# Loading x earlier, narrower first V products, matmuls on zeros and an earlier memory update in an attention and gMLP block on one core

## The chip, the cores and the metric

The kernel runs on one core of a Trainium2 chip. The metric is the device time of one execution in microseconds (us). Ratios are computed as the mean time of one kernel's runs over the mean of the other kernel's runs of the same rounds, so a ratio is not quite the ratio of the medians that are quoted beside it.

## The reference

The block has two halves. The first is attention with a compressive memory (32 heads of 32, four segments of 512 tokens); the second is a gMLP. The change touches the first half only.

```python
x = A_x                                   # 1 x 2048 x 1024, bfloat16
h  = x + attn(layernorm(x))               # below
h2 = h + gmlp(layernorm(h))               # gelu, layernorm, 2048x2048 spatial mix, w_out

# attn, per head; q, k, v = x @ wq, x @ wk, x @ wv, cut into 4 segments of 512
M, z = 0, 0
for s in range(4):
    logits = qs @ ks.T * scale + mask     # local, causal
    a_dot  = softmax(logits) @ vs
    a_mem  = phi(qs) @ M / (phi(qs) @ z + 1e-6)
    outs.append(g * a_mem + (1 - g) * a_dot)
    M = M + phi(ks).T @ vs                # the memory update
    z = z + phi(ks).sum(0)
return concat(outs) @ wo
```

## The kernel before

The kernel is written for five instruction streams (TensorE `pe`, ScalarE `act`, VectorE `dve`, GpSimd `pool`, SyncE `sp`, which issues all DMAs). A recorder derives every semaphore wait from the bytes and PSUM banks that an instruction touches. Each stream runs in program order, so the order in which the Python code calls things is the order in which each engine meets them. Each segment is worked off in eight iterations `c` of four heads; `n = 8 s + c`.

The prologue loads x and weights and prepares segment 0:

```python
x_load(0)
x_load(1)
sp.dma_start(WV[:, :, 0:512], wcols(A_wv, 0, 512))
x_load(2)
x_load(3)
sp.dma_start(WK[:, :, 0:256], ...)
sp.dma_start(WQ[:, :, 0:256], ...)
sp.dma_start(BETAB[:], ...)
sp.dma_start(WV[:, :, 512:1024], ...)
sp.dma_start(WK[:, :, 256:D], ...)
sp.dma_start(WQ[:, :, 256:D], ...)
sp.dma_start(WO[:], wcols(A_wo, 0, D))          # 2 MB, needed in segment 1
# ... cut ...
stats_of(0)                                     # bn_stats on DVE, rsqrt on POOL
stats_of(1)
for tc in range(4):
    o = ln_apply(XCH[tc], ks[tc])               # DVE
    if tc < 2:
        stats_of(tc + 2)
    pe_T(XNT[0], tc, o)                         # 8 transposes on PE, copy on ACT
    proj_v(0, tc, 0)                            # 8 matmuls 128x512, copy on ACT
gates()                                         # gate and MASKG, on DVE
proj_qk(0, 1); proj_qk(0, 0); phi(0)            # phi(n): DVE, then a DMA transpose into PK
rot["banks"] = [6, 7]                           # all fills below share two PSUM banks
```

The loop. `logits(n, r)` is four to eight small matmuls into banks 0 to 3 and an exp on ScalarE (`e_106`, `e_107`, `e_108` for r = 0, 1, 2). `fill` does whole projections of 8 matmuls (K and Q of the next iteration, V, or the output projection `wo` of the segment before); each takes the next bank of the two. `mem(n)` and `mem_norm(n)` (`rdm`, `tm`) read the memory inside the third logits. `state(n)` is the memory update:

```python
if s < NSEG - 1 and c < 4:
    x_load(4 * (s + 1) + c)                     # x of the next segment, used in this iteration
    ln_tasks(XCH[c], XNT[(s + 1) % 2], c)
logits(n, 0); fill(f1)                          # f1: K of n + 1
if n > 0: pv(n - 1, 2)                          # ends with norm(n - 1) on DVE
bg_pop()                                        # one step of up to three layer norms, on DVE
logits(n, 1); fill(f2)                          # f2: Q of n + 1
pv(n, 0)
logits(n, 2)                                    # with mem(n), mem_norm(n) from segment 1 on
fill(f3)
if n < LAST: phi(n + 1)
pv(n, 1)
bg_pop()
state(n)
fill(f4)                                        # empty in segment 0
bg_pop()

def state(n):                                   # not in the last segment
    b = next_bank()
    for tcl in range(4):
        pe.matmul(PS[:, b, 0:132], PK[n % 3][:, tcl, :], V[...], ...)
    dve ... MSUM[:, c, :] (+)= PS[:, b, 0:132]  # frees the bank
    dve ... MZB[:, c] = MSUM[:, c] * MASKG[:, c]
```

The softmax here doesn't subtract the row's maximum and nothing guards it: scores larger than these inputs give would overflow.

## Time and profile before

The median is 827.59 us (827.46 to 829.17). This is how the span of 825.4 us in its profiled execution divides, by the start of the first logits of an iteration in the timeline:

| stretch | from, us | length, us |
|---|---|---|
| prologue | 0 | 28.79 |
| iteration 0 | 28.79 | 7.62 |
| rest of segment 0 (n = 1 to 7) | 36.41 | 54.61 |
| segments 1 and 2 (n = 8 to 23) | 91.02 | 167.83 |
| segment 3 and the gMLP | 258.85 | 566.55 |

From the page of the kernel before, the span and the engines' busy time:

```profile
span 825.4 us, 12334 instructions
PE 787.2 (95%) x5258; PEld 384.3 (47%) x5344; DVE 368.6 (45%) x753; ACT 301.8 (37%) x351; POOL 120.8 (15%) x234
```

TensorE bounds the kernel as a whole; 38 us are left in which it is idle. What it waited for between 25 and 262 us, from the waits of PE (total us, times, longest; a line of 2.5 us called "issue" and lines of 0.7 us and less are left out):

```profile
PE ps L209 <- DVE hch_86 L209: 3.0, 3, 1.3
PE ps L209 <- DVE msum L209: 2.9, 5, 0.8
PE ps L209 <- DVE hch_87 L209: 2.7, 2, 1.9
PE ps L209 <- DVE hch_85 L209: 2.5, 3, 1.1
PE ps L209 <- ACT v L209: 1.1, 4, 0.3
```

All of the lines shown are waits for a PSUM bank that another engine has not emptied yet: `hch` is the residual add of the output projection, `msum` the update, `v` the copy of V. How such a wait comes about is seen in iteration 10. First TensorE, then VectorE, from the timeline (start, duration, what, and the idle time before it with its cause):

```profile
119.75 0.40 PE L209 MATMUL ps<-v,pk_104 128*128 128x132 bf16 x4
121.30 0.38 PE L209 MATMUL ps<-wo,oT 128*128 128x512 bf16 x1 [1.15 <-DVE hch_85 L209]
```

```profile
117.71 1.42 DVE L209 BATCH_NORM_STATS2 stats_61<-xch_94 128x6 f32<-128x512 bf16 x2 [1.08 <-DMA xch_94<-in_A_x_dram]
119.29 0.12 DVE L209 TENSOR_SCALAR rdm<-ps 128x16 f32<-128x16 f32 x1
119.73 0.69 DVE L209 TENSOR_TENSOR tm<-ps,rdm 128x512 f32<-128x512 f32 x1
120.34 0.68 DVE L209 TENSOR_TENSOR hch_85<-xr_83,ps 128x512 bf16<-128x512 bf16 x1
```

The second `wo` fill (121.30) has the bank of the first, because the update took the other one. The waits of DVE between 30 and 262 us:

```profile
DVE stats_60 L209 <- DMA xch_93<-in_A_x_dram: 7.7, 3, 3.6
DVE stats_59 L209 <- DMA xch_92<-in_A_x_dram: 7.6, 2, 5.0
DVE stats_61 L209 <- DMA xch_94<-in_A_x_dram: 5.5, 3, 3.2
DVE stats_62 L209 <- DMA xch_95<-in_A_x_dram: 3.1, 1, 3.1
```

### The profile page before, as it was taken

Reading aid. Unit: us, or ns where it says so; the run is one execution under the profiler, and the core shown is the slowest. Engines: PE = TensorE matmul, PEld = TensorE weight load, DVE = VectorE, ACT = ScalarE, POOL = GpSimd, SP = SyncE. Lnnn points to the kernel's source line nnn. Section 1 sums busy time; section 2 is a strip of 40 time slices with the busy share of each in tenths; the row PEclk is TensorE's granted clock in tenths of the full one; section 3 lists DMA queues with packets and bytes.
Section 4 is the critical chain, followed back from the end, with each engine's and each line's share of the span. In section 5 each row is a group of like instructions: output and inputs, shape, how many; then the busy total and the mean of one; then the engine's idle time right before and its main releaser. Section 6 shows DMA issues by size and latency. Waiting matters only on the chain.

```text
span 825.4 us, 12334 instructions
## 1 busy us (share of the span) xinstructions
PE 787.2 (95%) x5258; PEld 384.3 (47%) x5344; DVE 368.6 (45%) x753; ACT 301.8 (37%) x351; POOL 120.8 (15%) x234
## 2 busy tenths in 40 slices
PE   4899998998899999999999999999999999999998
PEld 2445444444444555455554444444444444444443
DVE  4454568756775568564456000043233314323432
ACT  2788866776667876133333333200000000000000
POOL 2143233323332233000033000000000000000000
PEclk9999999999999999999999999999999999999999
DMA  8631344344422224841013400190170035012002
GB/s 276 218 81 34 78 91 114 65 87 93 116 65 53 45 84 123 200 106 52 3 50 96 83 1 1 57 243 1 56 155 0 7 91 114 0 52 58 0 8 84
DMA packets 124808, 64.79 MB, mean 78 GB/s; under 512 B 94800, under 2 KB 113744, under 8 KB 124752
## 3 DMA queue, kind: packets, MB, share of 16 engines
q1 hardware_dynamic: 124752, 63.99, 31.2%
q8 instruction: 42, 0.69, 0.3%
q14 instruction: 14, 0.11, 0.1%
HBM read 32.51 MB, written 8.39 MB: 50 GB/s over the span
## 4 chain that ended last, share of the span: by engine, by line
PE 80%; DVE 9%; DMA 5%; ACT 3%; issue 2%; SPq 1%; POOL 0%
PE ps L209 80%; DMA xch_93<-in_A_x_dram 1%; DMA xch_95<-in_A_x_dram 1%; DMA xch_94<-in_A_x_dram 1%; DMA wv<-in_A_wv_dram 1%; ACT e_108 L209 1%; DVE stats_60 L209 1%; DVE stats_62 L209 1%; DVE rdm L209 1%; SPq L209 1%; ACT v L209 1%; DVE tm L209 1%; ACT etmp L209 1%; DVE etmp L209 1%; DVE stats_59 L209 1%
## 5 line engine op out<-in xcount | busy, mean ns | idle before, releaser
L209 PE MATMUL ps<-w_out,yT 128*128 128x512 bf16 x439 | 96.9, 379 | 0.5
L209 PE MATMUL ps<-wspT_119,z_117 128*128 128x512 bf16 x439 | 96.5, 379 | 0.5
L209 PE MATMUL ps<-wspT_120,z_117 128*128 128x512 bf16 x439 | 96.5, 379 | 0.5
L209 ACT ACTIVATE e_106<-ps 128x2048 bf16<-128x2048 f32 x32 | 60.0, 1874 | 36.2 <-PE ps L209 36.2
L209 PEld LDWEIGHTS ps<-wspT_119,z_117 128*128 128x128 bf16 x448 | 43.8, 98 | 52.8
L209 PEld LDWEIGHTS ps<-wspT_120,z_117 128*128 128x128 bf16 x448 | 43.8, 98 | 52.9
L209 PEld LDWEIGHTS ps<-w_out,yT 128*128 128x128 bf16 x448 | 43.8, 98 | 52.9
L209 PE MATMUL ps<-wo,oT 128*128 128x512 bf16 x243 | 57.2, 379 | 8.7 <-DVE hch_86 L209 3.0
L209 DVE TENSOR_TENSOR tmpg_126<-ps,brow_124 128x512 f32<-128x512 f32 x14 | 9.7, 690 | 117.6 <-DMA brow_124<-in_B_b_sp_dram 97.3
L209 ACT ACTIVATE z_117<-ps 128x448 bf16<-128x448 f32 x64 | 34.8, 544 | 74.7 <-PE ps L209 74.7
L209 ACT ACTIVATE e_107<-ps 128x2048 bf16<-128x2048 f32 x32 | 60.1, 1877 | 0.5 <-PE ps L209 0.5
L209 ACT ACTIVATE z1T<-ps 128x512 bf16<-128x512 f32 x56 | 33.4, 597 | 63.3 <-PE ps L209 63.3
L209 DVE BATCH_NORM_STATS2 zst<-z_117 128x6 f32<-128x448 bf16 x64 | 39.1, 620 | 32.6 <-ACT z_117 L209 32.6
L209 POOL TENSOR_SCALAR_AFFINE_SELECT e_107<-e_107 128x512 bf16<-128x512 bf16 x64 | 39.6, 643 | 46.9 <-ACT e_107 L209 46.9
L209 PEld LDWEIGHTS ps<-wo,oT 128*128 128x128 bf16 x256 | 23.6, 98 | 33.5 <-DVE hch_86 L209 3.3
L209 POOL TENSOR_SCALAR_AFFINE_SELECT e_106<-e_106 128x512 bf16<-128x512 bf16 x32 | 20.3, 634 | 126.9 <-ACT e_106 L209 126.9
L209 PE MATMUL ps<-wv,xnT_77 128*128 128x512 bf16 x121 | 30.5, 396 | 7.0 <-ACT xnT_77 L209 3.7
L209 ACT ACTIVATE e_108<-ps 128x1024 bf16<-128x1024 f32 x32 | 32.7, 1023 | 10.5 <-PE ps L209 10.3
L209 PE MATMUL ps<-xnT_78,wk 128*128 128x512 bf16 x125 | 29.7, 380 | 2.1 <-DVE msum L209 1.6
L209 ACT ACTIVATE v<-ps 128x512 bf16<-128x512 f32 x32 | 19.1, 597 | 34.4 <-PE ps L209 34.4
L209 PE MATMUL ps<-xnT_77,wk 128*128 128x512 bf16 x125 | 29.7, 380 | 2.0 <-DVE msum L209 1.3
L209 PE MATMUL ps<-xnT_77,wq 128*128 128x512 bf16 x120 | 28.8, 380 | 1.2 <-issue 0.8
(206 smaller groups left out, 1068.0 us busy)
## 6 DMA issues: line engine op xcount, KB each, us to landing
w_out<-in_B_w_out_dram SPq DMA_DIRECT2D x1, 3584.0 KB, 13.4
wv<-in_A_wv_dram SPq DMA_DIRECT2D x2, 1024.0 KB, 7.4
wo<-in_A_wo_dram SPq DMA_DIRECT2D x1, 2048.0 KB, 16.6
xr_83<-in_A_x_dram SPq DMA_DIRECT2D x8, 256.0 KB, 3.0
xr_84<-in_A_x_dram SPq DMA_DIRECT2D x8, 256.0 KB, 3.1
win_114<-in_B_w_in_dram SPq DMA_DIRECT2D x2, 896.0 KB, 5.5
wk<-in_A_wk_dram SPq DMA_DIRECT2D x1, 1536.0 KB, 10.0
wq<-in_A_wq_dram SPq DMA_DIRECT2D x1, 1536.0 KB, 12.8
```

The source lines that it names most:

```text
L209: ins = getattr(e, op.name)(*op.args, **op.kw)
```

## The change

It has four parts. The first V products are made in quarter widths and loaded so, with layer norms of chunks 0 and 1 ahead of later statistics, to start the first logits sooner; twelve matmuls on zeros run before any data is there, to raise TensorE's clock. (One early exp on ScalarE stands in the diff too; ScalarE's table load is at 0.79 us in both profiles.) x is loaded a segment ahead. The mask of the gates moves into iteration 0. And the update moves up, to right after the third logits, which also gives the two fills of an iteration different banks.

```diff
-    x_load(0)
-    x_load(1)
-    sp.dma_start(WV[:, :, 0:512], wcols(A_wv, 0, 512))
-    x_load(2)
-    x_load(3)
+    for tc in range(4):
+        x_load(tc)
+    sp.dma_start(WV[:, :, 0:256], wcols(A_wv, 0, 256))
+    sp.dma_start(WV[:, :, 256:512], wcols(A_wv, 256, 512))
 ...                                         (WK, WQ first 256 columns, BETAB, second half of WV)
-    sp.dma_start(WK[:, :, 256:D], ...)
-    sp.dma_start(WQ[:, :, 256:D], ...)
-    sp.dma_start(WO[:], ...)
 ...
+    dve.memset(ETMP[:], 0.0)
+    act.activation(RDM[:, 0, 0:1], MHALF[:], ACTF.Exp)
 ...
+    for i in range(12):
+        pe.matmul(bank(7), IDENT[:], ETMP[:, 0, :], start=True, stop=True)
     stats_of(0)
     stats_of(1)
+    late = {1: [(0, 0)], 2: [(1, 0)], 3: [(2, 0), (0, 1), (1, 1), (3, 0), (2, 1), (3, 1)]}
+    lns = [ln_apply(XCH[0], ks[0]), ln_apply(XCH[1], ks[1])]
     for tc in range(4):
-        o = ln_apply(XCH[tc], ks[tc])
         if tc < 2:
             stats_of(tc + 2)
-        pe_T(XNT[0], tc, o)
-        proj_v(0, tc, 0)
+        pe_T(XNT[0], tc, lns[tc])
+        if tc in (1, 2):
+            lns.append(ln_apply(XCH[tc + 1], ks[tc + 1]))
+        for t_, q in late.get(tc, []):
+            proj_v_cols(0, t_, 256 * q, 256)
+    for tc in range(4, 8):
+        x_load(tc)
+    sp.dma_start(WK[:, :, 256:D], wcols(A_wk, 256, D))
+    sp.dma_start(WQ[:, :, 256:D], wcols(A_wq, 256, D))
+    sp.dma_start(WO[:], wcols(A_wo, 0, D))
 ...
         if s < NSEG - 1 and c < 4:
-            x_load(4 * (s + 1) + c)
             ln_tasks(XCH[c], XNT[(s + 1) % 2], c)
+        if s < NSEG - 2 and c >= 4:
+            x_load(4 * (s + 2) + c - 4)
 ...
         logits(n, 2)
+        if n == 0:
+            mask_g()
+        else:
+            state(n)
         fill(f3)
 ...
         bg_pop()
-        state(n)
+        if n == 0:
+            state(n)
         fill(f4)
```

## The prediction

> **What bounds the kernel.** TensorE is busy 95% of 825.4 us (page, part 1). After 345 us no TensorE gap over 0.1 us is left and the change touches nothing there, so only the first 260 us count. Timeline and waits, by stage:
> - Prologue: first logits at 28.79 us. LN of chunk 1 waits in VectorE's order behind the statistics of chunk 2 (x chunk landing at 10.8), and first V waits 2.3 us for its 1 MB weight load. Matmuls at 10.27-13.2 are spaced 427 ns, from 15.7 on 216 ns[...].
> - Segment 0: 7.65 us an iteration, TensorE and ScalarE nearly tied (ScalarE idles 0.8 us, before the V copy). Iterations 2-4 take 7.9-8.1: VectorE waits for x chunks (2-5 us each), frees the PV banks late.
> - Segments 1 and 2: 83.7 and 84.1 us. TensorE waits for hch evacuation 8.2 us in 8 places (second output-projection half takes the bank of the first), for msum about 3 us, for v about 1 us.

> **What changes.**
> 1. Prologue compute. Quarter V, LN of chunks 0 and 1 before later statistics and warm-up matmuls: adding up the trace's durations (statistics 1.6, LN 0.5, transposed copy 1.0, warm quarter V 0.9) gives first logits near 23.4, 5.4 us earlier.
> 2. But the queue. Four x chunks (1 MB) now precede the rest of WK, WQ and WO, all before the transpose that the first memory update needs. Packets after 14 us move at about 380 GB/s; WO's last moved at 30.5. An extra 1.05 MB puts it at about 33.4, and the transpose, issued near 24.5, stands behind it. ([...]here a transpose issued at 338.1 shows no packets until the weight load ahead of it ended near 342.) It lands near 35, against 33.3 before, when the update ran at 36.1 without waiting. So TensorE stalls 4-5 us at the first update; iteration 1 starts near 35.6 against 36.41. Kept: 0.8 us[...].
> 3. x a segment ahead takes VectorE's x waits (27 us in all) away; TensorE gets about 1 us in segment 0, and part of item 4.
> 4. Update at the third logits. In segments 1-2 the two fills of an iteration get different banks, and the second waits for msum, whose chain (e_108 exp, rdm, tm, msum) ends 2.7 us after mem, 0.3 after TensorE is ready. Output-projection iterations 10.3-11.7 -> 9.9-10.4; V iterations unchanged to -0.35. Both segments together -6 us. In segment 0 ScalarE's V copy now comes 0.27 us later in a ScalarE-tied loop: 7.65 -> 7.9 in most iterations, +2 us.

> **Sum.** -0.8 + 0.6 - 1 - 6 + 2, about -5.5: predicted 822 us, 80% range 815.5 to 826.5. Chances: faster by over 2% 0.06, within 2% 0.93, slower 0.01.

> **Signs.** Right: logits near 23-24 us; a TensorE wait of 3-6 us on the pk transpose before iteration 1; iterations of segment 0 near 7.9; no hch waits of a microsecond in segments 1-2 but waits on msum of 0.2-0.4; segments near 81; no x wait on VectorE after 30 us. After 345 us everything shifted only.

> **What would make it wrong.** If the transpose overtakes WO, 5 us more are kept (about 817). If VectorE, with 10.0-10.5 us of work in iterations with two layer norms, falls behind, msum comes late and the segments gain only 2-3 us. If ScalarE's slack hides the moved update, 2 us more.

The allowance for TensorE's clock in the stall was not worked out from any trace. The sum keeps that allowance as its term +0.6: all five terms come to -5.2, and without it they come to -5.8. The predicted 822 us was made with it.

## The result, and the profile after

The changed kernel takes 822.00 us (820.99 to 823.47) against 827.53 in the same rounds; the ratio is 0.9931 (95% interval 0.9908 to 0.9955), within 2%. From its page:

```profile
span 819.4 us, 12417 instructions
PE 792.0 (97%) x5302; PEld 390.7 (48%) x5388; DVE 373.9 (46%) x754; ACT 302.6 (37%) x356; POOL 120.8 (15%) x234
```

| stretch | before, us | after, us | difference |
|---|---|---|---|
| prologue | 28.79 | 23.31 | -5.48 |
| iteration 0 | 7.62 | 12.00 | +4.38 |
| rest of segment 0 | 54.61 | 56.49 | +1.88 |
| segments 1 and 2 | 167.83 | 161.08 | -6.75 |
| segment 3 and the gMLP | 566.55 | 566.52 | -0.03 |

**The prologue's 5.5 us come back as a stall.** The waits of PE, 25 to 262 us, changed kernel:

```profile
PE ps L209 <- DVE msum L209: 4.7, 16, 0.4
PE ps L209 <- DMA pk_103<-pqk_99: 4.2, 1, 4.2
PE ps L209 <- ACT e_106 L209: 2.2, 8, 0.7
```

The second line is one wait, in TensorE's timeline at the end of iteration 0:

```profile
30.20 0.56 PE L209 MATMUL ps<-v,e_107 128*128 128x33 bf16 x16
34.98 0.40 PE L209 MATMUL ps<-v,pk_103 128*128 128x132 bf16 x4 [4.23 <-DMA pk_103<-pqk_99]
35.31 0.39 PE L209 MATMUL ps<-qk_97 32*128 32x512 bf16 x4
35.64 3.44 PE L209 MATMUL ps<-xnT_77,wk 128*128 128x512 bf16 x8
```

Iteration 1 starts at 35.31 us against 36.41 before: only 1.1 us are left. The DMA view of 14 to 36 us gives the time from issue to landing, first of the kernel before, then of the changed one:

```profile
wo<-in_A_wo_dram SPq DMA_DIRECT2D x1, 2048.0 KB, 16.6
pk_103<-pqk_99 SPq DMA_TRANSPOSE x1, 3.2
```

```profile
wo<-in_A_wo_dram SPq DMA_DIRECT2D x1, 2048.0 KB, 18.6
pk_103<-pqk_99 SPq DMA_TRANSPOSE x1, 10.3
```

The transpose was issued at 30.07 before and at 24.58 after. It landed at 33.3 and 34.9: issued 5.5 us sooner, it arrived 1.6 us later. WO, issued at 15.61, landed at 34.2 (15.61 + 18.6); before, at 31.5 (14.89 + 16.6), 1.4 us after the transpose was issued.

**After the stall the clock was at one half.** The last timeline line shows eight matmuls of 128x512 in 3.44 us, where the same group took 1.90 in other iterations. TensorE in stretches of 3.41 us, changed kernel (us, PE busy and instructions, granted clock, DMA share, GB/s):

```profile
5.11:8.52 3.41, 1.65 (x14) 1.00 1.04 309
8.52:11.94 3.42, 2.67 (x16) 0.50 1.20 291
32.41:35.83 3.42, 0.85 (x9) 1.00 0.54 74
35.83:39.24 3.41, 3.41 (x17) 0.50 0.43 84
```

**Segments 1 and 2.** No `hch` or `v` wait is left in the list; instead there are 16 short ones for `msum` (the first line of the waits above). The place shown before, iteration 10, on VectorE and then TensorE:

```profile
117.09 1.41 DVE L209 BATCH_NORM_STATS2 stats_61<-xch_94 128x6 f32<-128x512 bf16 x2
119.32 0.17 DVE L209 TENSOR_SCALAR rdm<-ps 128x16 f32<-128x16 f32 x1 [0.57 <-ACT e_108 L209]
120.42 0.28 DVE L209 TENSOR_TENSOR msum<-msum,ps 128x132 f32<-128x132 f32 x1
```

```profile
120.76 1.04 PE L209 MATMUL ps<-wo,oT 128*128 128x512 bf16 x4 [0.18 <-DVE msum L209]
```

The statistics no longer wait for x; VectorE now waits for `e_108`, which it needs for the memory read.

### The profile page after: what moved, and what is told of

Read it like the earlier page. It is cut to its first block, busy times and chain, and to the rows that moved or that the text cites. A ratio compares the mean times of both kernels' runs of the same rounds, so it can differ in the third digit from the quotient of the medians.

```text
span 819.4 us, 12417 instructions
## 1 busy us (share of the span) xinstructions
PE 792.0 (97%) x5302; PEld 390.7 (48%) x5388; DVE 373.9 (46%) x754; ACT 302.6 (37%) x356; POOL 120.8 (15%) x234
## 4 chain that ended last, share of the span: by engine, by line
PE 83%; ACT 8%; DVE 6%; issue 2%; DMA 2%; POOL 0%
PE ps L209 83%; ACT e_106 L209 3%; ACT e_108 L209 3%; DVE tm L209 2%; DMA pk_103<-pqk_99 1%; DVE rdm L209 1%; ACT v L209 1%; ACT etmp L209 1%; DVE stats_61 L209 0%; DVE stats_62 L209 0%; DVE msum L209 0%; DMA xch_92<-in_A_x_dram 0%; DVE hch_85 L209 0%; DVE etmp L209 0%; DVE lno_89 L209 0%
## 5 line engine op out<-in xcount | busy, mean ns | idle before, releaser
L209 ACT ACTIVATE z1T<-ps 128x512 bf16<-128x512 f32 x56 | 33.4, 597 | 63.3 <-PE ps L209 63.3
L209 PE MATMUL ps<-wv,xnT_77 128*128 128x512 bf16 (+1 forms) x154 | 29.8, 343 | 1.5 <-DVE msum L209 1.2
L209 ACT ACTIVATE v<-ps 128x512 bf16<-128x512 f32 (+1 forms) x36 | 19.8, 550 | 29.3 <-PE ps L209 29.3
L209 PE MATMUL ps<-wv,xnT_78 128*128 128x512 bf16 x120 | 28.5, 379 | 1.5 <-DVE msum L209 1.2
## 6 DMA issues: line engine op xcount, KB each, us to landing
wo<-in_A_wo_dram SPq DMA_DIRECT2D x1, 2048.0 KB, 18.6
```

The lines of the kernel that those rows point to most:

```text
L209: ins = getattr(e, op.name)(*op.args, **op.kw)
```

## The experiments

In the lines below from experiments the buffer numbers are missing from the tile names; `pk` is `pk_103` to `pk_105`, and so on. Stage lengths and start times are from one profiled execution of each kernel. The start of the first logits goes with the clock of that execution. In the four profiles with the old prologue (e3, before, e4, e10) it lies at 28.09, 28.79, 29.55 and 31.03 us, where the record of full clock begins at 13.85, 14.41, 18.49 and 19.93. In the six with the twelve zeros it lies between 23.31 and 25.04. e1, e2, e5 and e7 ran on one chip, e3, e4, e6 and e8 on another, e7_again, e9 and e10 together. Every kernel gave correct output.

The theories at the start: (Q) the prologue's gain is eaten by the order of the DMA queue; (S) in segment 0 the earlier update costs time, because ScalarE and TensorE are tied there; (B) the banks are what shortens segments 1 and 2. The rivals: the transpose is late for reasons of its own; 7.89 us has other causes; and the waits for x, not the banks, were the cost in segments 1 and 2.

### e1_wo_late: the changed kernel with WO behind the first transpose

```diff
-    sp.dma_start(WO[:], wcols(A_wo, 0, D))      # before gates()
 ...
     phi(0)
+    sp.dma_start(WO[:], wcols(A_wo, 0, D))
```

> The changed kernel, with the load of WO issued after the transpose that the first memory update waits for, instead of ahead of it. Theory (the queue keeps the order of issue, so the transpose stands behind 2 MB of WO): the transpose lands near 29 to 31 us instead of 35, the 4.23 us TensorE wait before the first update is gone or under 1 us, iteration 1 starts near 31 instead of 35.31 and stays at the full clock; time near 816.5, 5 to 6 us below the changed kernel. Rival (the transpose is late for its own reasons, such as the gates' mask work on VectorE or sharing of the DMA engines): the wait stays over 3 us and the time near 822.

Measured: 817.32 us (817.07 to 818.01) against 828.11, ratio 0.9874. From its DMA view of 14 to 36 us:

```profile
wo<-in_A_wo_dram SPq DMA_DIRECT2D x1, 2048.0 KB, 9.8
pk<-pqk SPq DMA_TRANSPOSE x2, 3.6
```

The wait before the first update is gone (iteration 0 takes 7.62 us). Iteration 1 starts at 32.62 us, not near 31, because in this profile the first logits came at 25.00 instead of 23.31; in it the granted clock is 0.50 from 12.31 to 15.72 us, see e9. Theory Q holds, its rival falls. The gain, about 4.7 us between the medians of the changed kernel and of e1 (817.32 and 822.00, different rounds), is a little under the 5 to 6 expected. All four executions of e1 have a mean granted clock of 0.998, so probably all of them had one such stretch (half of 3.41 us is 0.002 of the span of 815.8); that would explain the missing part. Of the two transposes in the view, the first took 3.3 us from issue to landing. The second, issued at 34.02, now stands behind WO, which landed at 37.4 (27.62 + 9.8); it landed at 38.0, and TensorE waits 0.21 us for it in iteration 1. A later transpose costs 0.36 us in iteration 7.

### e2_seg0_late: the update of segment 0 back at the end

```diff
         if n == 0:
             mask_g()
-        else:
+        elif s > 0:
             state(n)
 ...
-        if n == 0:
+        if s == 0:
             state(n)
```

> The changed kernel with the memory update of segment 0 back at the end of the iteration; segments 1 and 2 keep it at the third logits. Theory (ScalarE and TensorE are tied in segment 0, and the moved update delays the V copy by 0.27 us): iterations 2 to 7 return from 7.89 to 7.65 us, the time falls 1.5 to 2 us, to about 820.3. Rival (7.89 comes from other work, such as layer norms now running at other times): iterations stay near 7.9 and the time near 822.

Measured: 820.28 us (817.84 to 820.97), ratio 0.9904. Iterations 2 to 7 take 7.65 us each (42.87, 50.52, 58.17, ... us), as expected, against 7.89. The reason is visible in ScalarE's timeline. First the kernel before, iteration 5, then the changed kernel, iteration 5, then e2, iteration 5:

```profile
75.18 0.60 ACT L209 ACTIVATE v<-ps 128x512 bf16<-128x512 f32 x1 [0.80 <-PE ps L209]
```

```profile
75.74 0.60 ACT L209 ACTIVATE v<-ps 128x512 bf16<-128x512 f32 x1 [1.03 <-PE ps L209]
```

```profile
72.94 0.60 ACT L209 ACTIVATE v<-ps 128x512 bf16<-128x512 f32 x1 [0.79 <-PE ps L209]
```

This is the only larger idle time of ScalarE in such an iteration. In the changed kernel the update runs on TensorE before V, so V, its copy and everything after it on ScalarE come later, and TensorE then waits 0.23 us for `e_106` at the second logits. Theory S holds: the stages show it. (The profile is the fastest of four executions whose other three lie at 820.15 and above; its clock stayed up after the stall. Its transpose, issued at 26.32 us behind WO, took 8.5 us to land.)

### e5_old_start: the changed kernel with the old compute of the prologue

```diff
-    (12 matmuls on zeros, quarter-width V, lns ahead)
+    for tc in range(4):
+        o = ln_apply(XCH[tc], ks[tc])
+        if tc < 2:
+            stats_of(tc + 2)
+        pe_T(XNT[0], tc, o)
+        proj_v(0, tc, 0)
```

> The changed kernel with the compute of its prologue as in the kernel before (no matmuls on zeros, V of the first half at once, layer norms in the old order); the loads keep their new order. Theory (the queue sets the end of iteration 0): first logits 2 to 4 us later than 23.31, the wait for the transpose shrinks by as much, iteration 1 starts within 0.5 us of 35.31, and the time is 820.5 to 822.5, perhaps 1 us under the changed kernel, as a shorter wait leaves the clock up. Rival (the earlier start is kept in the end): 2 to 4 us slower than the changed kernel, 824 to 826.

Measured: 821.29 us (820.55 to 821.82), ratio 0.9921. The first logits come at 28.37 us, 5.1 us later than in the changed kernel (more than the 2 to 4 expected), the wait for the transpose vanishes, iteration 1 starts at 36.00 (0.7 us later than in the changed kernel; I had expected at most 0.5), and its clock stays up: from there to segment 1 it takes 54.97 us instead of 56.49.

```profile
35.67 0.40 PE L209 MATMUL ps<-v,pk 128*128 128x132 bf16 x4
```

Taking out the whole compute part of the new prologue does not make the kernel slower. The rival falls; together with e1 this shows that in the changed kernel the queue, and not the compute before it, decided when iteration 0 could end.

### e3_update_only and e4_x_only: one part each, on the kernel before

e3 is the kernel before with the placement of the update alone. e4 is the kernel before with x a segment ahead alone:

```diff
 e3:     logits(n, 2)
+        if n > 0:
+            state(n)
         fill(f3)
 ...
-        state(n)
+        if n == 0:
+            state(n)

 e4:     phi(0)
+        for tc in range(4, 8):
+            x_load(tc)
 ...
-            x_load(4 * (s + 1) + c)
             ln_tasks(XCH[c], XNT[(s + 1) % 2], c)
+        if s < NSEG - 2 and c >= 4:
+            x_load(4 * (s + 2) + c - 4)
```

> The kernel before with the placement of the memory update alone (third logits, except in iteration 0); x chunks still load in the iteration that uses them. Theory (the exchange of banks is what shortens segments 1 and 2, but msum is then behind the VectorE wait for x in the first four iterations of each): segments 1 and 2 take 81 to 82.5 us instead of 83.7 and 84.1, segment 0 grows by 1 to 2 us, time 824 to 826. Rival (the x waits were what cost the time, and the placement only helps with them gone): segments 1 and 2 stay within 1 us, time 828 to 830.

> The kernel before with x a segment ahead alone: chunks 4 to 7 are loaded after the first transpose and later ones in the second half of a segment; the update stays last and the prologue's loads and compute are as before. Theory: segment 0's iterations 2 to 4 return to 7.65 us (1 us gained); in segments 1 and 2 the hch waits stay, shortened from 1.2-1.9 to 0.6-0.8 us in the first two output-projection iterations, and msum waits stay in part; each segment gains 1 to 2 us; time 823.5 to 825.5. Rival (the bank exchange is all): segments 1 and 2 unchanged, time 826.5 to 827.

Measured: e3 830.81 us (829.31 to 834.89), ratio 1.0050 (1.0022 to 1.0078): slower than the kernel before. e4 821.41 us (821.12 to 822.55), ratio 0.9931 (0.9916 to 0.9946): the same ratio as the whole change. Both of my expectations missed, e3 by 5 us and e4 by 2, in opposite directions.

| | rest of segment 0, us | segments 1 and 2, us |
|---|---|---|
| before | 54.61 | 167.83 |
| e3, update alone | 57.80 | 167.40 |
| e4, x alone | 53.55 | 163.57 |
| after, both (with the new prologue) | 56.49 | 161.08 |

The update alone saves 0.4 us in segments 1 and 2. The waits of PE, 25 to 262 us, in e3, then in e4:

```profile
PE ps L209 <- DVE msum L209: 14.4, 19, 2.0
```

```profile
PE ps L209 <- DVE hch L209: 5.4, 8, 0.8
PE ps L209 <- DVE msum L209: 1.1, 2, 0.6
```

In e3 the `hch` waits are gone, as the exchange of banks intends, but longer waits for `msum` stand in their place. An example from iteration 11 of e3, VectorE, then TensorE:

```profile
132.43 1.42 DVE L209 BATCH_NORM_STATS2 stats<-xch 128x6 f32<-128x512 bf16 x2 [1.85 <-DMA xch<-in_A_x_dram]
135.06 0.28 DVE L209 TENSOR_TENSOR msum<-msum,ps 128x132 f32<-128x132 f32 x1
```

```profile
135.40 1.90 PE L209 MATMUL ps<-wo,oT 128*128 128x512 bf16 x8 [1.75 <-DVE msum L209]
```

With x late, VectorE is late for whatever bank it has to empty next, and moving the update only changes which bank that is. In segment 0 it even adds a wait: the K fill of iterations 2 to 4 waits 1.0 to 1.2 us for `msum`, which the old order did not put in front of it. With x early (e4) VectorE's own waits for x after 30 us fall to one of 4.2 us (26.5 us in e3), and both kinds of TensorE's wait shrink: `hch` from 8.2 us to 5.4, `msum` from 2.9 to 1.1. So theory B in its strong form falls, and so does its strong rival. The early x is the main part, and the placement of the update is worth something in segments 1 and 2 only on top of it: 163.57 to 161.08, 2.5 us.

### e6_both, e7_update_before_third and e8_no_zeros

e6 is e1 and e2 together. e7 is e6 with the update of segments 1 and 2 one place further up; the product with the mask has to stay behind the memory read, since it overwrites what that reads:

```diff
         pv(n, 0)
+        if s > 0:
+            state(n)                       # matmuls, and MSUM += on VectorE
         logits(n, 2)
         if n == 0:
             mask_g()
         elif s > 0:
-            state(n)
+            mzb(n)                         # MZB = MSUM * MASKG
```

e8 is e7 without the twelve matmuls on zeros.

> e1 and e2 together: WO behind the first transpose and the update of segment 0 at the end of the iteration. Theory (two separate causes that add up): 5 us from the queue and 1.7 from segment 0, time 815 to 816; against it e7 has the earlier update of segments 1 and 2 alone, so e7 should be 5 to 6 us below. Rival (with the stall gone the later start of segment 0 gives the rest back, and e7's gain is mostly elsewhere): 817 or more.

> e1 and e2 together, and in segments 1 and 2 the update's matmuls one place earlier, ahead of the third logits (the product with the mask stays behind them). Theory (each second fill there waits 0.3 us for msum behind the normalisation of the memory read): those 16 waits go, iterations of segments 1 and 2 fall from 9.93-10.08 to 9.65-9.8, and the time is about 810.5: 5.5 from the queue, 1.7 from segment 0, 4.5 from here. Rival (ScalarE or VectorE bounds those iterations as well): near 815, as the first two parts alone.

> e7 without the twelve matmuls on zeros. There is no stall in e7 that could hide the prologue, so what they are worth must show. Theory (they raise the clock before V's first products, though a cold stretch can come back in the gaps): first logits 1 to 2.5 us later than 23.34, time 810.5 to 812. Rival (the gaps of the prologue lower the clock again whatever came first, so they are worth nothing on average): within 0.5 us of e7's 809.5.

| kernel | median, us | lowest to highest | ratio to before (95%) | segments 1 and 2, us |
|---|---|---|---|---|
| e6 | 814.47 | 813.63 to 815.22 | 0.9848 (0.9831 to 0.9864) | 160.83 |
| e7 | 809.53 | 808.69 to 810.36 | 0.9779 (0.9764 to 0.9795) | 155.92 |
| e8 | 809.81 | 808.69 to 811.02 | 0.9789 (0.9774 to 0.9803) | 155.94 |

e6: the queue and segment 0 add up; it lies a little under the 815 to 816 expected. e7: iterations of segments 1 and 2 fall from between 9.93 and 10.08 us to between 9.59 and 9.74 (iterations 8, 12 and 20, where ScalarE or VectorE is late for another reason, from 10.63, 10.14 and 10.14 to about 10.06), and the 16 waits for `msum` are gone. What is left of the waits of PE, 25 to 262 us, in e7:

```profile
PE ps L209 <- ACT e L209: 0.6, 2, 0.4
PE ps L209 <- DVE ta L209: 0.6, 2, 0.3
PE ps L209 <- DVE tm L209: 0.4, 2, 0.2
```

e7 beats both kernels: it is faster than the kernel before by over 2%. In it, `msum` no longer stands on VectorE behind the memory read. In iteration 10 of the changed kernel that chain (exp on ScalarE, `rdm`, `tm`) had kept `msum` until 120.42 us, 2.4 us after the update's matmuls began at 118.06; in e7 `msum` starts 1.2 us after them (109.30 and 110.46), and the second fill starts without a wait. Iteration 10 of e7, VectorE, then TensorE:

```profile
110.46 0.24 DVE L209 TENSOR_TENSOR msum<-msum,ps 128x132 f32<-128x132 f32 x1
```

```profile
112.23 1.89 PE L209 MATMUL ps<-wo,oT 128*128 128x512 bf16 x8
```

e8's median is 0.3 us above e7's, in other rounds; the profile of e8 had its first logits at 25.65 us instead of 23.34. Its four executions were 808.69, 808.94, 810.68 and 811.02, those of e7 808.69, 808.71, 810.36 and 810.36. The zeros do raise the clock earlier in these two profiles: the record of full clock begins at 4.31 us in e7 and at 16.83 in e8, where eight matmuls of 128x256 at 9.36 us took 1.90 us against 1.03 in e7. But by the median they are worth nothing that four executions resolve, as the rival said; what makes two groups was open.

### e7_again, e9_more_zeros and e10_x_and_update

e9 is e7 with zeros in the prologue's gaps as well: 13 matmuls at the start, 3 after the first transposes, 4 after the first quarter of V. e10 is e4 with e7's placement of the update in segments 1 and 2, and the old prologue.

> e7 once more, unchanged, as the measure for the next two on the same chip: 809 to 810[...].

> e7 with 13 matmuls on zeros at the start, 3 more after the first transposes and 4 after the first quarter of V, in the gaps where the clock fell in the changed kernel's profile (8.5 to 11.9 us). Theory (the clock falls again in the prologue's gaps, in some executions, and that is what makes two groups): first logits at 23.3 to 23.8 in the profile without a cold stretch after the first 5 us, the slower group is gone, median 0.3 to 1 us under e7. Rival (the two groups come from elsewhere, or the added matmuls delay the real ones as much): median equal to e7 or up to 1 us above.

> The kernel before with x a segment ahead (as in e4) and with e7's placement of the update in segments 1 and 2; prologue, weight order and segment 0 as before. Theory: e4's 821.4 less the 7.6 us by which e7's segments 1 and 2 are shorter than e4's, so 813 to 815; the difference to e7, 4 to 5 us, is then what the changed prologue is worth once the transpose no longer stands behind WO. Rival (the gains overlap): over 816.

Cut from e7_again's expectation is that its executions may fall into two groups: the reason given was a mechanism that no run shows. The four executions of e7 above had shown the two groups, 1.65 us apart.

e7_again: 808.57, 808.65, 808.69 and 810.34 us. Its profile fell on the last of these, with the first logits at 24.99 us. e9: 808.65, 808.65, 808.71, 808.74 and 808.84; first logits at 23.38; ratio 0.9776 (0.9763 to 0.9790). TensorE in stretches of 3.41 us, e7_again, then e9, then e6:

```profile
9.30:12.72 3.42, 1.40 (x18) 1.00 1.20 290
12.72:16.13 3.41, 3.41 (x23) 0.50 1.11 344
```

```profile
8.05:11.47 3.42, 2.80 (x23) 1.00 1.20 290
11.47:14.88 3.41, 2.82 (x34) 1.00 1.13 319
```

```profile
8.36:11.77 3.41, 1.49 (x16) 1.00 1.20 291
```

In e7_again the clock falls to 0.50 for one stretch of 3.41 us in the middle of the prologue, after one with 1.40 us of work. That delays the first logits by 1.65 us against e7's profile (24.99 and 23.34), and the two executions differ by as much (810.34 and 808.69). In both e7 jobs the slow executions are just those with a mean granted clock under 1 (0.997 and 0.998), three of eight. In e6, whose prologue is the same, the clock stayed up in the profile after a stretch with 1.49, less than the 1.65 after which it fell in the changed kernel: busy time in the stretch before does not settle it alone. e1 has this prologue too: all four executions of e1 and the slower two of e6 show 0.998 as well, so nine of sixteen executions with this prologue lost clock. With work in the gaps, e9's slow group is gone in five executions, all with a clock of 1.0, though its median is the same as e7_again's (808.71 and 808.67). So the theory of the two groups holds for e7, as far as five executions show it (e8's groups are not explained); a lower median, which I had expected, did not come, because three of four executions of e7_again were already in the fast group.

e10: 814.83 us (813.58 to 816.39), ratio 0.9851, as expected. Its segments 1 and 2 take 155.94 us, as in e7. Against e7_again of the same rounds the new prologue, once WO no longer stands in front of the transpose, is worth about 6 us by the medians and 5 by the fastest executions (4 to 5 expected). In the change's own profile it was 5.5 us at the first logits, of which 1.1 were left at iteration 1.

## Why the prediction was right or wrong

The time was predicted at 822 us (815.5 to 826.5) and came out at 822.00. Taken apart, some steps were right; the gains from early x and from the update were mis-sized, in opposite directions, and nearly cancelled. That the median is 822.00 is therefore partly luck; the prediction's own terms add up to -5.2, not to the -5.5 that it rounds to, and the measured ones to -6.0.

| step of the prediction | predicted, us | shown by |
|---|---|---|
| first logits | near 23.4 | 23.31 (about 25 in e1, e2 and e7_again, by the clock) |
| stall on the transpose, start of iteration 1 | 4 to 5; 35.6 | 4.23; 35.31 |
| clock after the stall | +0.6 | +1.5 (56.49 after, 54.97 in e5); +1.3 by iteration 1 alone (9.17, 7.91 in e1) |
| x a segment ahead | -1 "and part of item 4" | -5.3 alone (e4: -1.06 in segment 0, -4.26 in 1 and 2) |
| update: segments 1 and 2 | -6 | -2.5 on top of x (163.57 to 161.08); -0.4 alone (e3) |
| update: segment 0 | +2 | +1.4 on top of x (53.55 in e4, 54.97 in e5); +3.2 alone |

The measured terms add up to the change of the span: -5.48 + 4.38 (iteration 0) + 1.52 (clock) - 5.32 (x) - 2.49 + 1.42 (update) = -5.97 us, and 825.4 less 819.4 is 6.0.

*Right:* the queue. The prediction estimated from bytes and rate that WO's last bytes would move at 33.4 us and that the transpose would land near 35. That the transpose waits behind WO rested on one place in the kernel before: a transpose issued at 338.08 us, behind a weight load of 896 KB issued at 337.65, landed 5.7 us later, and packets under 512 B, the transposes' size in that profile, are absent from 338.5 us and begin again at about 341.8. e1 (3.3 us from issue to landing without WO in front), e5 (first logits 5.1 us later, iteration 1 only 0.7) and the 10.3 us here agree.

*Right:* the tie of ScalarE and TensorE in segment 0 (e2), the short `msum` waits of 0.2 to 0.4 us, and that nothing but a shift happens after segment 2.

*Wrong:* the step "Update at the third logits ... Both segments together -6 us". I took the `hch` and `msum` waits of the kernel before as the price of the bank order, and put down only about 1 us to the x waits, "and part of item 4". The runs showed the reverse: of the 6.75 us measured there, 4.26 come with early x alone, and the bank order alone gives 0.4. The total of segments 1 and 2 (predicted near 81 each, measured 80.8 and 80.3) was right because I had worked out the state with both parts in place. It said nothing on which part did it. By the words "and part of item 4" early x had a share in the 6 us, but the text booked them under the update, and e3's expectation shows that I took the update for the main part. The trace had the hint: VectorE's line at 117.71 waits for x before the chain that TensorE then waits for.

*Undersized:* the clock. I allowed 0.6 us as a chance; the half-clock stretch that followed cost 1.3 to 1.5 in the profile.

## What to carry to other kernels

Ask of every load that you move forward which small transfer now stands behind it in the same queue: a small DMA that an engine will wait for (here a transpose of 128 x 512 bfloat16: 10.3 us from issue to landing behind 2 MB of WO, 3.3 in e1 ahead of it) should be issued before bulk weights that nobody needs for 100 us. When two parts of a change meet in one wait, the engine named last in the wait tells only half; try each part alone, since here the plain one (load earlier) alone gave as much as the whole change and the clever one (exchange the banks) made things worse until the other was there. And in a loop where two engines are tied, work that is moved earlier on one of them delays the other: place the update where its result is not behind an unrelated chain (e7), and only in the stretches where the other engine has slack (e2).
